# A new order table for a two-layer linear-attention and gated-GLU kernel, with the masks and the activation-table load moved in its first microseconds

## The chip, the cores and the metric

One core of a Trainium2 chip runs the whole program. The metric is device time in microseconds (us) of one execution. The kernel before took 378.02 us (median of three runs, 377.85 to 378.40).

## The reference

The input `x` is 2048 rows of 512 bfloat16 numbers. Four stages follow one another, each added to its own input: A, B, A, B, with the same weights both times.

```
x = x + A(layernorm(x));  x = x + B(layernorm(x));  x = x + A(layernorm(x));  x = x + B(layernorm(x))

A: q, k, v = x @ wqkv                       # 32 heads of 16
   phi(u)  = [softmax(u @ w_phi), softmax(-(u @ w_phi))]      # 32 features a head
   kv = sum over s of phi(k)^T v;   z = sum over s of phi(k)
   o  = (phi(q) kv) / (phi(q) z + 1e-6);    result = o @ wo
B: result = (relu(x @ W_gate) * (x @ W_up)) @ W_down          # width 1376
```

## The kernel before, in words

The 2048 rows are 16 tiles of 128 rows by 512, held in `X` on the chip for the whole run; four tiles make a chunk. The work on one tile is a chain of small operations over five engines: TensorE (PE) multiplies, VectorE (DVE), ScalarE (ACT) and GpSimd (POOL) do what lies between, SyncE (SP) issues transposing DMAs and loads. All line numbers are those of the kernel before; in the changed kernel the lines of the functions shown here stand 7 to 35 further down, those of the key and query stages 33.

**Stage A of layer 0, keys.** A layernorm's statistics are `bn_stats` and `bn_aggr` on DVE (L331, L333), some 128x2 operations on POOL (L339, L341, L389, L391: the power to -1/2 is L341), and the normalising operation on ACT (L403), DVE or POOL (L415). The normalised tile is transposed. PE makes `k` through `w_phi` (L653, four matmuls) and `v` (L606). ACT takes the exponential of + and - of it (L674) into `ek`. The sums of each head's features come from DVE alone (L625 over both halves, L635 over one), or from POOL adding one half's pairs first (L622, here called a half) and DVE the rest (L631). DVE inverts the sums (L683, `rk`). Then `ek` is multiplied by `rk` (L688, here called the scale): a table `ks` says for each tile how many of its eight groups of four heads POOL does, the rest is DVE's. So a tile of 128x1024 elements is one operation on one of these engines, or one on each. PE sums the scaled features times `v` over all 16 tiles (L711). After the last tile DVE masks the result into `R` (L733, two operations).

**Queries and outputs.** Queries go the same way (L753, L757, sums at L622 to L635, L762, L766, a scale at L773, a transposing DMA at L775). When `R` stands, PE multiplies each query tile by it (L792, called er here); its result has one buffer, so each er waits until DVE has read the one before (L810 and L812). The output is transposed (by PE at L832, or by DMA), multiplied by `wo` (L843) and added to `X` (L509). Nothing of stage B starts before that.

**Stage B** takes gate and up (L556), the activations (L562 to L573), a rest of 96 columns (L536 to L546), the down product (L588) and the addition to `X` (L513). In layer 0 each finished tile goes straight into the statistics, the keys and the queries of layer 1, so the stages overlap.

**What sets the order.** Python builds one list of 1881 operations in program order (`Plan.op`). `ORDER`, a table of 1881 numbers written into the file, says in what order they are given out (`emit`). Each engine runs its own share of that list strictly in that order, and waits at an operation until its inputs are there and its buffer is free. The table `STEP` says by a letter or a digit which engine does an operation. Numbers such as `occ`, `lat` and `at` in `Plan.op` do not reach the chip.

**The start.** Two loads of `X` are issued on SP, five loads on ACT's queue (`LOAD_ACT`), then the activation that makes ACT load its exponential table (L172). Until the first statistics DVE fills constants. The masks `M8` and `M4` (L198, L200) are made from constants that POOL prepares; `M8` is needed for the block-diagonal `Wblk` (L270), `M4` for `R`. PE multiplies zeros 20 times (L261), then transposes and folds the key weights (L294, L307), which ACT or DVE copies out (L250, L252, table `wev`).

Of the kernel before, what the change touches and what calls it, by code (L numbers as in the profile page):

```python
# [8 lines left out]
P = 128  # L9
D = 512  # L10
# [7 lines left out]
EPS = 1e-5  # L18
# [32 lines left out]
class Plan:  # L51
# [65 lines left out]

NV = 8
# [3 lines left out]
WF_IN, WK_IN, WV_IN, WQ_IN, LOADED = 3.5, 5.95, 10.0, 14.1, 13.0  # L122
X_IN = [3.27, 3.85] + [7.2] * 2 + [8.5] * 4 + [11.4] * 4 + [12.8] * 4
# [8 lines left out]
def setup(ctx, tc, A_x, A_wqkv, A_w_phi, A_wo, B_W_gate, B_W_up, B_W_down, out):  # L132
# [32 lines left out]
    for what in LOAD_ACT:  # L165
        load(nc.scalar, what)
# [5 lines left out]
    nc.scalar.activation(out=wake[:], in_=st.zero[:, 0:1], func=AF.Exp)  # L172
    M8f = const.tile([P, 8], F32, name="M8f")
# [24 lines left out]
    nc.vector.tensor_copy(out=M8[:], in_=M8f[:])  # L198
    st.M4 = const.tile([P, 4], BF16, name="M4")
    nc.vector.tensor_reduce(out=st.M4[:], in_=ident[:].rearrange("p (k h) -> p h k", h=4), axis=AX.X, op=Alu.max)  # L200
# [45 lines left out]
def evacuate(st, eng, ends, on_dve, **deps):  # L246

    nc, pl = st.nc, st.pl
    if eng == "A":
        pl.op("ACT", 0.475, lambda: nc.scalar.copy(out=ends()[0], in_=ends()[1]), **deps)  # L250
    else:
        pl.op("DVE", on_dve, lambda: nc.vector.tensor_copy(out=ends()[0], in_=ends()[1]), **deps)  # L252

# [59 lines left out]
class Norm:  # L313
# [8 lines left out]
    def add(self, t):  # L322
# [8 lines left out]
        pl.op("DVE", 0.597, dur=0.69, fn=lambda: nc.vector.bn_stats(out=bn[:], in_=st.X[:, t, :]), reads=[("X", t)] + ([("Xin", t)] if self.at else []), writes=[(bn, 0)],  # L331
# [448 lines left out]
def attention(st, c, pT, norm, L):  # L780
# [72 lines left out]
    "tB0": "A---", "tB1": "---A", "tA": "----", "wev": "DDDAAAAADDDAAAAA", "xn1": "APAPDAADPAAPAAAA",  # L853
    "turn": "AAADDAAD", "wake": 20, "fuse0": "AFAA", "fuse1": "FFFF", "gate": 3, "sA": 3, "xB0": "ADAADDDADDDAAAAA",
# [5 lines left out]
}  # L860
ORDER = [int(i) for i in """
# [119 lines left out]
def kernel(  # L981
# [4 lines left out]
    with tc.manual_schedule():  # L986
        st.pl.emit()
# [30 lines left out]
```

## Time and profile before

| | us |
|---|---|
| runs: median (lowest, highest) | 378.02 (377.85, 378.40) |
| the profiled execution, its time | 377.86 |
| its span, first to last instruction | 376.1 |
| PE busy | 368.5 |
| DVE busy | 262.5 |
| ACT busy | 212.5 |
| POOL busy | 136.5 |

The profiled execution is 0.16 us under the median, and 1.76 us of it lie outside the span. The granted TensorE clock is 0.999 throughout. A row of the timeline gives the start and the length of an instruction, or of several of one kind in a row (x2, x3); in brackets is how long the engine was idle before it and what it waited for. Neighbouring rows of DVE overlap by 0.06 to 0.1 us, so a length is slightly more than the place it takes. A row of the waits says which line of which engine waited for whom: the total, how often, the longest.

### The profile page before, as it was taken

How to read it: one execution, taken by the hardware profiler on the slowest of the kernel's cores; microseconds unless marked ns; L12 is line 12 of the kernel's file. 1: busy time of each engine (PE TensorE's matmuls, PEld its weight loads, DVE VectorE, ACT ScalarE, POOL GpSimd, SP SyncE). 2: the span in 40 equal slices, each digit the busy share in tenths (PEclk: the TensorE clock that was granted, in tenths of full speed). 3: DMA queues.
4: the chain of work that ended last, by engine and by line, in shares of the span. 5: the costliest groups of instructions: out<-in, count | busy, mean ns of one | idle time of the engine just before them, and what ended most of it. 6: DMA issues, size and time to landing. Idle time of an engine off the chain costs nothing.

```text
span 376.1 us, 6927 instructions
## 1 busy us (share of the span) xinstructions
PE 368.5 (98%) x2530; PEld 196.6 (52%) x2530; DVE 262.5 (70%) x608; ACT 212.5 (57%) x478; POOL 136.5 (36%) x223
## 2 busy tenths in 40 slices
PE   8999998999999999999999999999999999999996
PEld 4455445877644545444444446566655454444453
DVE  7999999998879854267554976898875353325343
ACT  4999898767745537784666264786522352042100
POOL 6999998362410028024601765431410011000000
PEclk9999999999999999999999999999999999999999
DMA  8898565675843823400140032266583321000031
GB/s 267 178 194 186 139 147 99 116 108 120 133 93 63 120 43 71 98 0 2 29 92 7 15 58 44 49 121 127 119 136 84 58 62 24 0 14 2 0 110 60
DMA packets 95746, 31.83 MB, mean 85 GB/s; under 512 B 87424, under 2 KB 95200, under 8 KB 95712
## 3 DMA queue, kind: packets, MB, share of 16 engines
q1 hardware_dynamic: 93024, 27.97, 38.4%
q10 hardware_dynamic: 2688, 3.42, 2.7%
q8 instruction: 20, 0.33, 0.4%
q14 instruction: 14, 0.11, 0.1%
HBM read 8.44 MB, written 2.10 MB: 28 GB/s over the span
## 4 chain that ended last, share of the span: by engine, by line
PE 83%; DVE 12%; ACT 1%; DMA 1%; POOL 1%; issue 1%
PE ps L556 37%; PE ps L588 20%; PE ps L843 7%; PE ps L753 4%; PE ps L653 4%; PE ps L536 3%; PE ps L606 3%; DVE b L688 3%; PE q L792 2%; DVE sk L625 2%; DVE rk L683 2%; PE ps L261 1%; DVE sk L635 1%; DMA b<-b 1%; PE q L711 1%; DVE bnst L331 1%
## 5 line engine op out<-in xcount | busy, mean ns | idle before, releaser
L566 ACT ACTIVATE b<-ps 128x512 bf16<-128x512 f32 (+3 forms) x110 | 50.4, 482 | 68.1 <-PE ps L556 67.8
L556 PE MATMUL ps<-b,wu 128*128 128x512 bf16 (+3 forms) x440 | 82.1, 321 | 0.2 <-ACT sq L491 0.2
L556 PE MATMUL ps<-b,wg 128*128 128x512 bf16 (+3 forms) x440 | 81.5, 321 | 0.0
L588 PE MATMUL ps<-wd,b 128*128 128x512 bf16 (+4 forms) x374 | 79.2, 366 | 0.0
L588 PEld LDWEIGHTS <-b 128*128 128x128 bf16 (+1 forms) x374 | 35.3, 98 | 39.3
L556 PEld LDWEIGHTS <-wg 128*128 128x128 bf16 x440 | 38.5, 98 | 31.6
L556 PEld LDWEIGHTS <-wu 128*128 128x128 bf16 x440 | 38.4, 98 | 31.0 <-issue 0.5
L622 POOL TENSOR_TENSOR b<-b 128x256 f32<-128x256 bf16 x39 | 27.5, 718 | 62.8 <-ACT b L757 33.5
L569 DVE SCALAR_TENSOR_TENSOR b<-ps,b 128x512 bf16<-128x512 f32 (+2 forms) x60 | 34.1, 593 | 22.6 <-PE ps L556 12.2
L757 ACT ACTIVATE b<-ps 128x512 bf16<-128x512 f32 x64 | 37.3, 642 | 8.9 <-PE ps L753 7.6
L674 ACT ACTIVATE b<-ps 128x512 bf16<-128x512 f32 x64 | 37.7, 645 | 5.9 <-PE ps L653 5.4
L688 POOL TENSOR_TENSOR b<-b,rk 128x1024 bf16<-128x1024 bf16 (+6 forms) x26 | 36.7, 1424 | 7.5 <-DVE rk L683 4.4
L513 DVE SCALAR_TENSOR_TENSOR X<-ps,r,X 128x512 bf16<-128x512 f32 (+2 forms) x22 | 14.9, 694 | 27.7 <-PE ps L588 27.7
L653 PE MATMUL ps<-Wk,b 128*128 128x512 bf16 x128 | 32.2, 379 | 0.6 <-ACT b L250 0.3
L843 PE MATMUL ps<-wo,b 128*128 128x512 bf16 x128 | 32.7, 379 | 0.0
L753 PE MATMUL ps<-Wq,b 128*128 128x512 bf16 x128 | 32.0, 379 | 0.0
L606 PE MATMUL ps<-wkv,b 128*128 128x512 bf16 x128 | 31.8, 379 | 0.0
L509 DVE SCALAR_TENSOR_TENSOR X<-ps,X 128x512 bf16<-128x512 f32 x32 | 21.7, 679 | 7.4 <-PE ps L843 7.4
L562 ACT ACTIVATE b<-ps 128x128 bf16<-128x128 f32 (+2 forms) x50 | 20.5, 430 | 8.9 <-PE ps L556 8.4
L573 DVE TENSOR_TENSOR b<-b,b 128x128 bf16<-128x128 bf16 (+2 forms) x50 | 15.0, 332 | 14.8 <-ACT b L562 9.8
L773 POOL TENSOR_TENSOR b<-b,rq 128x512 bf16<-128x512 bf16 x21 | 22.1, 1056 | 0.7
L812 DVE TENSOR_TENSOR b<-q,dd 128x512 bf16<-128x512 f32 x32 | 21.8, 683 | 0.6
(94 smaller groups left out, 482.7 us busy)
## 6 DMA issues: line engine op xcount, KB each, us to landing
out_dram<-X SPq DMA_DIRECT2D x15, 128.0 KB, 1.9
X<-in_A_x_dram ACTq DMA_DIRECT2D x3, 512.0 KB, 6.6
b<-b SPq DMA_TRANSPOSE x91, 3.1
wg<-in_B_W_gate_dram SPq DMA_DIRECT2D x8, 160.0 KB, 2.7
wu<-in_B_W_up_dram SPq DMA_DIRECT2D x8, 160.0 KB, 3.2
wd<-in_B_W_down_dram SPq DMA_DIRECT2D x5, 256.0 KB, 3.2
wkv<-in_A_wqkv_dram ACTq DMA_DIRECT2D x2, 512.0 KB, 5.9
wq<-in_A_wqkv_dram ACTq DMA_DIRECT2D x1, 512.0 KB, 4.0
```

Source lines behind the costliest of these rows:

```text
L556: nc.tensor.matmul(ps[:], lhsT=wt[:, b, f * P:(f + 1) * P], rhs=xnT[:, lo:hi, b, :], start=(b == 0), stop=(b == NDB - 1))
L566: pl.op("ACT", 0.045 + 0.43 * share, lambda ups=ups, ru=ru, sign=1.0 if fuse else -1.0: nc.scalar.activation(out=ru[:], in_=ups[:], func=A ...
L569: pl.op("DVE", 0.058 + 0.548 * share, dur=0.138 + 0.548 * share, fn=lambda gps=gps, ru=ru, h=h, cs=cs: nc.vector.scalar_tensor_tensor(out= ...
L588: nc.tensor.matmul(yps[:], lhsT=hs[f][:fsz, ti * P:(ti + 1) * P], rhs=st.wd[:fsz, f, cols], start=(f == 0), stop=(f == NFT - 1))
L606: nc.tensor.matmul(vp[:], lhsT=xnT[:, ti, kb, :], rhs=st.wkv[:, kb, D:2 * D], start=(kb == 0), stop=(kb == NDB - 1))
L622: nc.gpsimd.tensor_tensor(out=h[:].rearrange("p j h f -> p j f h"), in0=x[:, :, 0], in1=x[:, :, 1], op=Alu.add)
L653: nc.tensor.matmul(ps[:], lhsT=xnT[:, ti, kb, :], rhs=w(kb), start=(kb == 0), stop=(kb == NDB - 1))
L674: pl.op("ACT", 0.48, lambda s=s, ek=ek, pk=pk: nc.scalar.activation(out=ek[:, :, s, :], in_=pk[:].rearrange("p (j x) -> p j x", j=8), func ...
L688: eng.tensor_tensor(out=phiK[:, lo:hi, :, :].rearrange("p j s (f h) -> p (j s) f h", h=4), in0=ek[:, lo:hi, :, :].rearrange("p j s (f h) - ...
L753: nc.tensor.matmul(pq[:], lhsT=xnT[:, ti, kb, :], rhs=st.Wq2[:, kb, :], start=(kb == 0), stop=(kb == NDB - 1))
L757: pl.op("ACT", 0.48, lambda s=s, eq=eq, pq=pq: nc.scalar.activation(out=eq[:, :, s, :], in_=pq[:].rearrange("p (j x) -> p j x", j=8), func ...
L843: nc.tensor.matmul(yps[:], lhsT=turned(b), rhs=st.wo[:, b, :], start=(b == 0), stop=(b == NDB - 1))
```

## The change

`ORDER` is a new table, now of 1885 numbers: the same operations in another order, with the two masks as operations in it. As numbers it tells a reader nothing. The replay is able to add waits between operations, from a table `BEHIND`; that table is empty, so none is added. The masks come ahead of the first `bn_stats`, which now names `M4` as an input. Three loads stay ahead of the table load on ACT's queue (f, k and tiles 2 and 3), two come behind it (tiles 4 to 7, v). `STEP` has changes in five entries, and a new entry `st` whose other letter, "A", no tile uses. The landing times are numbers of the planning only.

```diff
-    def emit(self):
+    def emit(self, tc):
         for o in self.order():
...
             o.fn()
+            o.ins = tc.nc.cur_bb.bb.instructions[-1]
+            for v in BEHIND.get(o.i, ()):
+                tc.add_manual_dep(o.ins, self.ops[v].ins.name, mybir.DependencyInfo(mybir.DependencyClass.Sync, mybir.DependencyReason.ANTI),
+                                  reason="one at a time on the port that VectorE and GpSimd share")
...
+BEHIND = {}
...
-    for what in LOAD_ACT:
+    for what in LOAD_ACT[:3]:
         load(nc.scalar, what)
...
     nc.scalar.activation(out=wake[:], in_=st.zero[:, 0:1], func=AF.Exp)
+    for what in LOAD_ACT[3:]:
+        load(nc.scalar, what)
...
-    nc.vector.tensor_copy(out=M8[:], in_=M8f[:])
-    nc.vector.tensor_reduce(out=st.M4[:], in_=ident[:].rearrange("p (k h) -> p h k", h=4), axis=AX.X, op=Alu.max)
...
+def masks(st):
...
+    pl.op("DVE", 0.1, lambda: nc.vector.tensor_copy(out=st.M8[:], in_=st.M8f[:]), writes=[("M8", 0)], at=2.75)
+    pl.op("DVE", 0.17, lambda: nc.vector.tensor_reduce(
+        out=st.M4[:], in_=st.ident[:].rearrange("p (k h) -> p h k", h=4), axis=AX.X, op=Alu.max), reads=[("M8", 0)], writes=[("M4", 0)], at=2.75)
...
-    "tB0": "A---", "tB1": "---A", "tA": "----", "wev": "DDDAAAAADDDAAAAA", "xn1": "APAPDAADPAAPAAAA",
+    "tB0": "A---", "tB1": "---A", "tA": "----", "wev": "ADADAAAADDDAAAAA", "xn1": "APAPDAADPAAPAAAA",
-    "turn": "AAADDAAD", "wake": 20, "fuse0": "AFAA", "fuse1": "FFFF", "gate": 3, "sA": 3, "xB0": "ADAADDDADDDAAAAA",
+    "xB0": "ADAAADAADADADADD", "xB1": "DDAAAAAAAADDDDAD", "xA": "ADDADDADDDDAADAD", "xm0": "11222111",
-    "xB1": "DDAAAAAAAADDDDAD", "xA": "ADDADDDADAADADAD", "xm0": "11222111", "xmB0": "12221222", "xmB1": "22121122",
-    "ks0": "6087060714860850", "ks1": "3484716308718788", "kr0": "2H2P11H11PH21HH1", "kr1": "21221HP12P1H212H",
+    "ev0": "AAAAAAAAAAAAAAAA", "ev1": "DAAAAAADAAAAADAD", "ks0": "6087160714860850", "ks1": "3484716308718788",
-    "qr0": "P2H1H2HPPH2P2H12", "qr1": "21P2111HHH2P1H1P", "qs0": "PPPPPPPPDPDDPDPP", "qs1": "DDPDDPDPPPPPDPDP",
+    "qs0": "PPPPPPPPPPDPPDPP", "qs1": "DDPDDPDPPPPPDPDP", "qq0": "PPPPPPPPPPDPPPPP", "qq1": "DDPDPDDDPPPPDPPP",
...
-3 4 5 108 109 110 111 112 113 114 115 116 117 118 7 6 138 8 134 0 9 12 13 14 15 129 128 139 135 16 130 142 131 140
+3 4 5 6 110 111 112 113 114 7 9 8 10 115 116 117 118 119 120 121 14 136 140 15 130 131 132 16 17 21 137 0 144 11 12 1
...
 def layers(st):
     NC, pl = st.NC, st.pl
     load_weights(st)
+    masks(st)
```

Three places show what the table moves. A name such as `b_409` is a buffer, with a number of its own in each program; `sk` are sums, `rk` their inverses.

The first place is on DVE, in the keys of layer 0, before: the scale of tile 3 (`b_428`, 128x128, the seven other parts being POOL's), then those of tile 6 (`b_475`) and tile 5 (`b_505`).

```order
L683 RECIPROCAL rk_749<-sk_533 128x64
L688 TENSOR_TENSOR b_428<-b_427,rk_611 128x128
L683 RECIPROCAL rk_762<-sk_711 128x64
L688 TENSOR_TENSOR b_475<-b_474,rk_749 128x1024
L688 TENSOR_TENSOR b_505<-b_504,rk_762 128x256
```

The same place of DVE in the change: tile 3's scale (`b_409`), the sums of tile 5, tile 6's scale (`b_469`), and tile 4's (`b_428`), which POOL now shares.

```order
L716 RECIPROCAL rk_664<-sk_510 128x64
L721 TENSOR_TENSOR b_409<-b_408,rk_618 128x128
L658 TENSOR_REDUCE sk_713<-b_500 128x64
L721 TENSOR_TENSOR b_469<-b_468,rk_664 128x1024
L721 TENSOR_TENSOR b_428<-b_427,rk_512 128x896
```

Tile 5's scale has left this place; tile 4's, which before stood eight places ahead of tile 3's, now stands behind tile 6's. On POOL the scale of all of tile 2 stood behind tile 3's; it now stands ahead of it.

The second place is some 10 us later, on DVE before: the scales of tile 8 (`b_639`), tile 7 (`b_542`) and tile 9 (`b_555`).

```order
L683 RECIPROCAL rk_818<-sk_801 128x64
L635 TENSOR_REDUCE sq_816<-b_647 128x8x4
L688 TENSOR_TENSOR b_639<-b_638,rk_811 128x896
L762 RECIPROCAL sq_816<-sq_816 128x8x4
L688 TENSOR_TENSOR b_542<-b_541,rk_809 128x128
L631 TENSOR_REDUCE sq_847<-b_709 128x8x4
L688 TENSOR_TENSOR b_555<-b_554,rk_818 128x512
```

On DVE in the change: tile 8 (`b_585`), tile 5 (`b_501`), tile 7 (`b_522`), a sum, tile 9 (`b_609`).

```order
L716 RECIPROCAL rk_757<-sk_752 128x64
L795 RECIPROCAL sq_750<-sq_750 128x8x4
L721 TENSOR_TENSOR b_585<-b_584,rk_747 128x896
L721 TENSOR_TENSOR b_501<-b_500,rk_723 128x256
L721 TENSOR_TENSOR b_522<-b_521,rk_734 128x128
L668 TENSOR_REDUCE sq_847<-b_634 128x8x4
L721 TENSOR_TENSOR b_609<-b_608,rk_757 128x512
```

POOL at the second place in the change: its parts of tile 7 (`b_522`), tile 5 (`b_501`) and tile 8 (`b_585`), halves (L655), and the scale of query tile 0 (`b_602`).

```order
L721 TENSOR_TENSOR b_522<-b_521,rk_734 128x896
L721 TENSOR_TENSOR b_501<-b_500,rk_723 128x768
L655 TENSOR_TENSOR b_759<-b_700 128x8x8x4
L799 TENSOR_TENSOR rq_805<-sq_750 128x32
L721 TENSOR_TENSOR b_585<-b_584,rk_747 128x128
L806 TENSOR_TENSOR b_602<-b_602,rq_805 128x8x64
```

So at the second place three scales of DVE now stand one behind the other and a fourth behind one sum, beside POOL's parts of the same tiles; before it was three scales, with a short operation between each two.

The third place is on DVE where layer 0 ends: tile 13's addition to `X` (`ps_3443`), its statistics, and its normalising operation (`b_3484`), before.

```order
L513 SCALAR_TENSOR_TENSOR X<-ps_3443,r_3039,X 128x512
L331 BN_STATS bnst_3465<-X 128x6
L333 BN_AGGR mv_3467<-bnst_3465 128x2
L762 RECIPROCAL sq_3459<-sq_3459 128x8x4
L688 TENSOR_TENSOR b_2915<-b_2914,rk_3094 128x256
L766 TENSOR_TENSOR rq_3477<-sq_3459 128x32
L415 TENSOR_SCALAR b_3484<-X,mv_3467,rstd_3473 128x512
```

In the change tile 13's addition (`ps_3383`) comes ahead of tile 14's (`ps_3397`).

```order
L546 SCALAR_TENSOR_TENSOR X<-ps_3383,r_3131,X 128x512
L364 BN_STATS bnst_3409<-X 128x6
L546 SCALAR_TENSOR_TENSOR X<-ps_3397,r_3131,X 128x512
L366 BN_AGGR mv_3420<-bnst_3409 128x2
L364 BN_STATS bnst_3475<-X 128x6
L658 TENSOR_REDUCE sq_3477<-b_3269 128x64
L721 TENSOR_TENSOR b_3281<-b_3280,rk_3328 128x896
L366 BN_AGGR mv_3480<-bnst_3475 128x2
L448 TENSOR_SCALAR b_3482<-X,mv_3420,rstd_3473 128x512
```

PE follows the same order: before, tile 13's down product was the last of layer 0; now it is the last but one, with tile 14's 11 matmuls behind it. Between tile 13's down product and its key product (L653) PE had 8 key and value products of four matmuls and 8 matmuls of L711 before; in the change it has tile 14's down product, 10 key and value products and 16 matmuls of L711.

More of the change, by code (lines that the diff above doesn't have):

```diff
@@ L121 @@
 LATE = ((8, 12), (12, 16), "q")
-WF_IN, WK_IN, WV_IN, WQ_IN, LOADED = 3.5, 5.95, 10.0, 14.1, 13.0
-X_IN = [3.27, 3.85] + [7.2] * 2 + [8.5] * 4 + [11.4] * 4 + [12.8] * 4
+WF_IN, WK_IN, WV_IN, WQ_IN, LOADED = 3.57, 5.83, 10.1, 14.03, 13.0
+X_IN = [3.35, 4.26] + [6.46] * 2 + [8.61] * 4 + [11.37] * 4 + [12.62] * 4
 TINY = 0.165
@@ L252, in evacuate @@
         pl.op("DVE", on_dve, lambda: nc.vector.tensor_copy(out=ends()[0], in_=ends()[1]), **deps)
+def masks(st):
+    nc, pl = st.nc, st.pl
+    pl.rank("w")
+    pl.op("DVE", 0.1, lambda: nc.vector.tensor_copy(out=st.M8[:], in_=st.M8f[:]), writes=[("M8", 0)], at=2.75)
+    pl.op("DVE", 0.17, lambda: nc.vector.tensor_reduce(
+        out=st.M4[:], in_=st.ident[:].rearrange("p (k h) -> p h k", h=4), axis=AX.X, op=Alu.max), reads=[("M8", 0)], writes=[("M4", 0)], at=2.75)
 def wake(st):
@@ L329, in add @@
             return self.add_sums(t, n)
+        by_act = self.at is not None and n == 1 and STEP["st"][t] == "A"
+        if by_act:
+            e2, nv, rstd = Buf("u", [P, 4], F32), Buf("ve", [P, 4], F32), Buf("rstd", [P, 4], F32)
+            for out, func, scale in ((lambda: e2[:, 0:1], AF.Square, D ** -0.5), (lambda: mv[:, 0, 0:1], AF.Identity, 1.0 / D)):
+                junk = Buf("sq", [P, D], BF16)
+                pl.op("ACT", 0.67, lambda out=out, func=func, scale=scale, junk=junk: nc.scalar.activation(
+                    out=junk[:], in_=st.X[:, t, :], func=func, scale=scale, accum_out=out()),
+                    reads=[("X", t), ("Xin", t)], writes=[(junk, 0), (e2, 0) if func == AF.Square else (mv, 0)], at=self.at[t])
+            pl.op("POOL", TINY, lambda: nc.gpsimd.tensor_scalar(
+                out=nv[:, 0:1], in0=mv[:, 0, 0:1], scalar1=mv[:, 0, 0:1], scalar2=e2[:, 0:1], op0=Alu.mult, op1=Alu.subtract),
+                reads=[(mv, 0), (e2, 0)], writes=[(nv, 0)])
+            pl.op("POOL", TINY, lambda: nc.gpsimd.tensor_scalar(
+                out=nv[:, 0:1], in0=nv[:, 0:1], scalar1=-1.0, scalar2=EPS, op0=Alu.mult, op1=Alu.add), reads=[(nv, 0)], writes=[(nv, 0), ("stat", t)])
+            pl.op("POOL", 0.39 + 0.155, lambda: nc.gpsimd.tensor_tensor(out=rstd[:, 0:1], in0=nv[:, 0:1], in1=st.mhalf[:, 0:1], op=Alu.pow),
+                  reads=[(nv, 0)], writes=[(rstd, 0)])
+            self.tiles.append(t)
+            return self.normalise(n, mv, rstd)
         bn = Buf("bnst", [P, 6], F32)
-        pl.op("DVE", 0.597, dur=0.69, fn=lambda: nc.vector.bn_stats(out=bn[:], in_=st.X[:, t, :]), reads=[("X", t)] + ([("Xin", t)] if self.at else []), writes=[(bn, 0)],
+        pl.op("DVE", 0.597, dur=0.69, fn=lambda: nc.vector.bn_stats(out=bn[:], in_=st.X[:, t, :]), reads=[("X", t)] + ([("Xin", t), ("M4", 0)] if self.at else []), writes=[(bn, 0)],
               at=self.at[t] if self.at else 0.0)
@@ L852 @@
     "raw": 0, "kev": "ADAD", "pp0": "1111111111111111", "pp1": "1111111111111111", "part0": "3111", "part1": "6111",
-    "tB0": "A---", "tB1": "---A", "tA": "----", "wev": "DDDAAAAADDDAAAAA", "xn1": "APAPDAADPAAPAAAA",
-    "turn": "AAADDAAD", "wake": 20, "fuse0": "AFAA", "fuse1": "FFFF", "gate": 3, "sA": 3, "xB0": "ADAADDDADDDAAAAA",
[5 rows of a table removed]
+    "tB0": "A---", "tB1": "---A", "tA": "----", "wev": "ADADAAAADDDAAAAA", "xn1": "APAPDAADPAAPAAAA",
+    "st": "DDDDDDDDDDDDDDDD", "turn": "AAADDAAD", "wake": 20, "fuse0": "AFAA", "fuse1": "FFFF", "gate": 3, "sA": 3,
[6 rows of a table added]
 }
 ORDER = [int(i) for i in """
[72 rows of a table removed]
[72 rows of a table added]
 """.split()]
@@ L986 @@
     with tc.manual_schedule():
-        st.pl.emit()
+        st.pl.emit(tc)
 _INS = ['A_x', 'A_wqkv', 'A_w_phi', 'A_wo', 'B_x', 'B_W_gate', 'B_W_up', 'B_W_down']
```

147 rows, old and new, of tables (ORDER, STEP) are left out of this document.

## The prediction

> **What bounds the kernel now.** First the page's busy shares, the windows by stage, and the waits of PE.
>
> ```profile
> PE 368.5 (98%) x2530; PEld 196.6 (52%) x2530; DVE 262.5 (70%) x608; ACT 212.5 (57%) x478; POOL 136.5 (36%) x223
> ...
> 15.00:60.00 45.00, 42.91 (x338) 22.41 (x336) 44.39 (x88) 41.70 (x82) 42.17 (x55) 1.00 0.71 150
> ...
> 80.00:220.00 140.00, 140.00 (x825) 72.22 (x823) 96.74 (x237) 83.55 (x192) 45.46 (x88) 1.00 0.34 63
> ...
> PE q L711 <- POOL b L688: 1.1, 2, 0.9
> ...
> PE q L792 <- DVE R L733: 0.3, 1, 0.3
> PE ps L653 <- ACT b L250: 0.3, 1, 0.3
> ```
>
> The columns of a window are its length, then the busy time of PE, PE's weight loads, DVE, ACT and POOL. PE is busy 368.5 of 376.1 us, so no order of the same matmuls can win more than the 7.6 us between them. The stages differ. From 80 to 220 us PE has no idle time at all: what DVE, ACT and POOL do there costs nothing while it comes in time. From 15 to 60 us DVE is busy 44.39 of 45 us, PE 42.91: there **DVE is the bound**. All keys of layer 0 must be scaled before `R`, and PE has no work that could go ahead of the first er without limit. So a microsecond more on DVE before `R` is a microsecond more at the end, and one less is a gain until PE's idle time there is used up, 45.00 - 42.91 = 2.1 us and the piece of the wait for L250 at 10.6, some 2.4 together.
>
> Inside those 45 us DVE's work is itself stretched. These are rows of the timeline of DVE, then of POOL.
>
> ```profile
> 26.35 1.16 DVE L688 TENSOR_TENSOR b<-b,rk 128x1024 bf16<-128x1024 bf16 x1
> ...
> 27.77 0.28 DVE L688 TENSOR_TENSOR b<-b,rk 128x256 bf16<-128x256 bf16 x1
> ...
> 28.75 0.62 DVE L688 TENSOR_TENSOR b<-b,rk 128x1024 bf16<-128x1024 bf16 x1
> ...
> 30.88 0.15 DVE L688 TENSOR_TENSOR b<-b,rk 128x128 bf16<-128x128 bf16 x1
> ...
> 31.42 2.54 DVE L688 TENSOR_TENSOR b<-b,rk 128x1024 bf16<-128x1024 bf16 x2
> ...
> 40.06 1.48 DVE L688 TENSOR_TENSOR b<-b,rk 128x896 bf16<-128x896 bf16 x1
> ...
> 41.73 0.42 DVE L688 TENSOR_TENSOR b<-b,rk 128x128 bf16<-128x128 bf16 x1
> ...
> 42.41 0.95 DVE L688 TENSOR_TENSOR b<-b,rk 128x512 bf16<-128x512 bf16 x1
> ...
> 54.50 1.55 DVE L688 TENSOR_TENSOR b<-b,rk 128x1024 bf16<-128x1024 bf16 x2
> ...
> 58.13 0.77 DVE L733 TENSOR_TENSOR R<-M,q 128x272 bf16<-128x272 bf16 x2
> ```
>
> ```profile
> 25.49 1.48 POOL L688 TENSOR_TENSOR b<-b,rk 128x768 bf16<-128x768 bf16 x1
> ...
> 31.04 1.69 POOL L688 TENSOR_TENSOR b<-b,rk 128x896 bf16<-128x896 bf16 x1
> 32.70 1.12 POOL L622 TENSOR_TENSOR b<-b 128x256 f32<-128x256 bf16 x1
> 33.77 1.96 POOL L688 TENSOR_TENSOR b<-b,rk 128x1024 bf16<-128x1024 bf16 x1
> ...
> 44.68 1.05 POOL L773 TENSOR_TENSOR b<-b,rq 128x512 bf16<-128x512 bf16 x1
> ```
>
> A whole tile's scale takes DVE 0.62 us alone (28.75). The same took 1.16 at 26.35, when POOL's scale of 25.49 ran until 26.97, and the pair at 31.42 took 2.54 where 0.62 + 0.28 = 0.90 would do, less 0.08 of overlap. DVE's scale ends about half a microsecond after the POOL operation it met: it **waits for it**. It goes the other way too: the half at 32.70 took 1.12, as it lay beside the end of DVE's first scale, and held up the second. The excess over the lone lengths is 0.54 at 26.35, 1.72 at 31.42, 0.9 at 40.06 (lone about 0.55, seven eighths of 0.62), 0.27 at 41.73, 0.6 at 42.41 (lone about 0.35) and 0.73 at 54.50 (a pair of 1024 and 256 again): 4.8 us in all.
>
> The Trainium skill, on the page "SBUF — State Buffer" under "Who interferes with whom", says that a DVE operation with two inputs in this memory and a GpSimd one that reads it share a port pair, held by whoever issues first for its whole instruction. The rows above agree for long POOL operations; the rivals come back to it.
>
> **The change part by part.** The sum is made against the profiled execution (377.86 us), 0.16 under the median.
>
> *Nothing: the waits.* The table from which `emit` would add waits is empty; what DVE waited for POOL before was the hardware's doing, and it stays so.
>
> *Masks.*
>
> ```profile
> 3.38 0.69 DVE L331 BATCH_NORM_STATS2 bnst<-X 128x6 f32<-128x512 bf16 x1 [0.60 <-DMA X<-in_A_x_dram]
> ...
> 5.12 0.25 DVE L200 TENSOR_REDUCE M<-ident 128x4 bf16<-128x128 bf16 x1
> 5.29 0.16 DVE L198 CAST M<-M8f 128x8 bf16<-128x8 f32 x1
> ...
> 6.58 1.18 DVE L252 COPY b<-ps 128x512 bf16<-128x512 bf16 x3 [0.34 <-PE ps L294]
> ...
> 1.47 0.19 POOL L177 TENSOR_SCALAR_AFFINE_SELECT M8f<-M8f 128x8 f32<-128x8 f32 x1
> ```
>
> Both take 0.41 us, fit into DVE's idle 0.60 before the first tile lands, and POOL has their inputs ready at 1.66. DVE gets 0.4 us earlier to `Wblk`, then waits 0.4 longer for PE's transposes at 6.58: I take 0. Without that cover it is worth -0.4 to +0.1. One copy of the weights goes from DVE to ACT, where that engine waits too: the bounds are the one L250 wait of PE gone (-0.3) or doubled (+0.3), 0 taken.
>
> *Table load between the issues.*
>
> ```profile
> 3.63 1.28 ACT L172 ACT_TABLE_LOAD   x1 [3.63 <-issue]
> 3.70 0.47 ACTq L162 DMA_DIRECT2D X<-in_A_x_dram  x1
> 5.99 0.81 ACT L403 ACTIVATE b<-X,ve,rstd 128x512 bf16<-128x512 bf16 x1 [0.86 <-POOL ve L391]
> ```
>
> A load was issued at 3.70 while the table load ran, so the table load doesn't hold the queue, and ACT's first real work waits for POOL until 5.99. With the load of v and tiles 4 to 7 behind the wake-up instead of ahead of it, the worst is one 1.28 us delay of tiles 4 to 7, whose statistics DVE reaches late enough to lose about 0.3 of it. I take 0, bounds 0 and +0.3.
>
> *The order of layer 0's keys.* DVE's operations ahead of `R` are the same in number and kind but for those just told and one small eighth of tile 4 that POOL takes, and PE has 406 matmuls ahead of the first er in both orders, so what can differ is how long scales wait. I followed both engines' new rows with the lone lengths above and the rule that a scale waits for the POOL operation running, and a waiting one goes first when the other ends:
> - tile 0's quarter on DVE now comes while POOL does its own three quarters (1.48, released by the same reciprocal): 1.2 us, between 0.9 and 1.48. Before, tile 0's quarter at 27.77 met nothing, and tile 4's paid 0.54.
> - tile 6 meets the tail of tile 2's 1.96 on POOL: 0.75, between 0 and 1.96; tile 4 behind it nothing, and a DVE sum idles 0.4 for a half that POOL starts later. Before, the two scales here paid 1.72.
> - tile 8 waits 0.2 for POOL's 1.69 to end. Then POOL's three quarters of tile 5 (1.48), waiting, go ahead of DVE's quarter of tile 5: 1.45. Tile 7's eighth waits for the half behind (0.65), and tile 9 for tile 0's query scale (1.05): 0.95. Together 3.25, between 1.0 if DVE's three go in one run and 4.4 if each meets a whole operation. Before: 0.9 + 0.27 + 0.6 = 1.8.
> - tiles 12, 14, 11 and 15: POOL's last scales are done by then: 0, up to 1. Before: 0.73.
>
> After: 1.2 + 0.75 + 0.4 + 3.25 = 5.6. Before: 4.8. **+0.8**, between -2.4 (PE's idle time, the most that can be won) and +3 (next part). `R` then starts near 58.9 instead of 58.13.
>
> *60 to 220 us.* The new letters move whole operations of 0.3 to 0.8 us between DVE and ACT. PE's 140.00 of 140 covers them, DVE having 43 us and ACT 56 us to spare in that window: 0. If the cover failed at one place it would be one such length, +0.8.
>
> *The end of layer 0.* PE's row with the stall, and how tile 13 came to it:
>
> ```profile
> 214.56 2.54 PE L588 MATMUL ps<-wd,b 128*128 128x512 bf16 x11
> ...
> 217.13 0.75 DVE L513 SCALAR_TENSOR_TENSOR X<-ps,r,X 128x512 bf16<-128x512 f32 x1 [0.44 <-PE ps L588]
> ...
> 219.98 0.41 DVE L415 TENSOR_SCALAR b<-X,mv,rstd 128x512 bf16<-128x512 bf16 x1 [0.67 <-POOL rstd L341]
> ...
> 222.37 1.03 PE L653 MATMUL ps<-Wk,b 128*128 128x512 bf16 x4
> 223.23 1.03 PE L606 MATMUL ps<-wkv,b 128*128 128x512 bf16 x4
> 224.49 1.04 PE L653 MATMUL ps<-Wk,b 128*128 128x512 bf16 x4 [0.23 <-DMA b<-b]
> ...
> 240.72 0.43 PE L792 MATMUL q<-R,b 128*128 128x68 bf16 x8 [0.31 <-DVE b L812]
> ```
>
> From tile 13's down product (ends 217.1) to its key product 7.4 us pass, and PE had only 8 products in between, at 0.86 each (222.37 to 223.23), and 8 short matmuls (0.3): the key product could have started at 223.23 + 0.86 = 224.09 and started at 224.49, a stall of 0.4 (0.23 of it shown as idle). Now PE has a down product (2.4), 10 products (8.6) and 16 short matmuls (0.5) there, 11.5 us, so the chain is hidden with 4 us to spare: **-0.4**. Tile 14, now last, has about 10 us of work behind it. Bounds -0.4 and 0. The stall at 240.72 stays: one er waits for the output of the one before, with one product between them; its neighbours change places, and I find about the same 0.5 again. Behind 256 us PE has only stage B: 0.
>
> **Sum:** 377.86 + 0.8 - 0.4 = 378.26; against the median 0.16 more, **378.4**.
>
> **The rivals.** A measurement of this kernel can tell about 0.2% (0.76 us) from no change.
>
> *The waits fall kindly (faster).* The list of waits is a guess at who comes first, each time by a few tenths. If the scales of tiles 8, 5 and 7 run in one piece, and tile 0's waits little, 1.6 to 3.2 us of the 5.6 go, the last of them at the limit of PE's idle time: -0.8 to -2.4 in front, -0.4 behind, 375.2 to 376.8. For it: these three stand together now, so that a POOL operation may be waited for once instead of three times. Against: POOL is itself busy 42.17 of 45 us, so a DVE scale that meets no POOL operation is rare.
>
> *A whole POOL scale in the wrong place (slower).* In the change tile 2's scale on POOL (1024 wide, 1.96) stands ahead of tile 3's, and tile 3's eighth on DVE (0.15 alone) comes at nearly the same time. If POOL is first, DVE waits up to 1.96 with everything behind it, and up to 1.1 more where a half slips in as at 32.70: +1.9 to +3. It decides within some 0.3 us of arrival. Then 380.3 to 381.4. For it: POOL has 1 us more to do than before ahead of tile 14's scale (a half more, and tile 4's eighth), so it comes later to all that stands behind. Against: in my walk DVE comes first.
>
> *Short POOL operations block too (slower by less).*
>
> ```profile
> 14.95 0.40 DVE L415 TENSOR_SCALAR b<-X,mv,rstd 128x512 bf16<-128x512 bf16 x1
> 14.91 0.71 POOL L341 TENSOR_TENSOR rstd<-ve,mhalf 128x2 f32<-128x2 f32 x1
> ```
>
> Here DVE took its usual 0.40 beside POOL's power of 0.71, so such operations seem not to block. That DVE row has one wide input, though, the scale two. If the scale does wait, tile 4's comes upon the power that now follows tile 2's scale: +0.7, 379.1. The same section of the Trainium skill would have it so, as it makes no difference of length; on the row above that rule does not hold.
>
> *The order does nothing.* If both orders lose the same in waits and the stall at 224 turns up elsewhere: 377.8 to 378.3.
>
> **How the numbers follow.** Forecast 40% (377.2 to 379.6: 0.03 faster, 0.20 same, 0.17 slower); kind waits 25% (faster); POOL's whole scale 20% and the short operations 8% (slower); nothing 7% (same). So 0.28 faster, 0.27 same, 0.45 slower. The range reaches half into the kind waits and nearly through the slow case: 376.0 to 381.3, which leaves out about 2 in 10.
>
> **What would show it.** Right: `R` on DVE starting at 58.5 to 59.5; a long tile 5 quarter near 41 (1.7 instead of 0.28); PE in the window 15 to 60 about 42 busy; no DMA wait at L653's successor. Wrong: `R` before 58 (kind waits), a 128x128 scale of 2 us near 30 (POOL first), a PE wait between 80 and 220, or the first key product after 11.2.

## The result, and the profile after

The changed kernel takes 376.63 us (median of 17 runs), the kernel before 378.09 (17 runs): a ratio of 0.9967, 95% interval 0.9958 to 0.9975, so 1.2 us faster by the ratio of the means (1.5 by the medians), and clear of no change. The forecast was 378.4, 0.1% slower. The time lies inside the stated range, but on the other side. A few executions of the study took 481 to 1375 us, among them the profiled ones of experiments 1 and 12; no ratio and no reading below rests on them.

The changed kernel's windows, and all waits of its PE:

```profile
15.00:60.00 45.00, 42.72 (x334) 22.02 (x332) 43.73 (x87) 41.27 (x81) 41.78 (x55) 1.00 0.68 154
...
80.00:220.00 140.00, 140.00 (x831) 72.44 (x829) 99.35 (x234) 82.32 (x192) 46.99 (x89) 1.00 0.35 62
PE q L744 <- DVE b L721: 1.7, 1, 1.7
PE ps L277 <- DVE zero L177: 1.2, 1, 1.2
PE ps L323 <- DVE b L259: 0.5, 1, 0.5
PE ps L639 <- ACT b L707: 0.3, 1, 0.3
PE ps L865 <- DVE b L845: 0.3, 1, 0.3
```

The front looks as before: DVE nearly full, PE 2.3 us short of the window. What is missing from the list are the small waits of the back: no key product waits for a DMA, no er for the output before it, no up product (L556 before) for ACT. (In the front, PE's waits at L711 of 1.1 and 0.6 have become one of 1.7.)

Three landmarks in PE's timeline divide the run: the first er of layer 0, the first er of layer 1, and the end. Of before, then of the change:

```profile
59.04 0.41 PE L792 MATMUL q<-R,b 128*128 128x68 bf16 x8 [0.29 <-DVE R L733]
...
235.15 0.43 PE L792 MATMUL q<-R,b 128*128 128x68 bf16 x8
```

```profile
58.94 0.41 PE L825 MATMUL q<-R,b 128*128 128x68 bf16 x8
...
234.41 0.41 PE L825 MATMUL q<-R,b 128*128 128x68 bf16 x8
```

| stretch | before | change | measured | forecast |
|---|---|---|---|---|
| start to first er, layer 0 | 59.04 | 58.94 | -0.10 | +0.8 |
| to first er, layer 1 | 176.11 | 175.47 | -0.64 | -0.4 |
| to the end (376.1, 374.8) | 140.95 | 140.39 | -0.56 | 0 |

The gain isn't where the forecast looked for a loss. It lies behind `R`, in stalls of PE of 0.1 to 0.5 us each. The rows of the last stretch, before (up to the er at 240.72) and in the change:

```profile
239.38 1.02 PE L843 MATMUL ps<-wo,b 128*128 128x512 bf16 x4
```

```profile
239.48 1.03 PE L786 MATMUL ps<-Wq,b 128*128 128x512 bf16 x4
240.35 0.42 PE L825 MATMUL q<-R,b 128*128 128x68 bf16 x8
...
241.46 0.39 PE L511 MATMUL ps<-ident,b 128*128 128x128 bf16 x4
241.94 0.43 PE L825 MATMUL q<-R,b 128*128 128x68 bf16 x8
```

Before, the er at 240.72 could have started 0.86 after the product at 239.38, at 240.24: a stall of 0.48. Now the er at 240.35 has an earlier product ahead of it and starts on time; the next has four transposes (0.22) more between, and stalls 241.94 - 241.68 = 0.26. And the stall of an up product at 253 is gone:

```profile
252.71 0.38 PE L556 MATMUL ps<-b,wg 128*128 128x128 bf16 x4
253.25 1.46 PE L556 MATMUL ps<-b,wu 128*128 128x384 bf16 x8 [0.15 <-ACT sq L491]
```

```profile
251.73 0.39 PE L589 MATMUL ps<-b,wg 128*128 128x128 bf16 x4
251.95 0.81 PE L589 MATMUL ps<-b,wu 128*128 128x384 bf16 x4
```

In the row of before 0.54 us lie between the starts where the change needs 0.22: 0.32. Together 0.22 + 0.32 = 0.54 of the 0.56.

**The key scales.** DVE's rows of the change that answer to those of the prediction, then POOL's:

```profile
25.72 0.97 DVE L721 TENSOR_TENSOR b<-b,rk 128x256 bf16<-128x256 bf16 x1
...
28.81 0.16 DVE L721 TENSOR_TENSOR b<-b,rk 128x128 bf16<-128x128 bf16 x1
...
30.01 2.12 DVE L721 TENSOR_TENSOR b<-b,rk 128x1024 bf16<-128x1024 bf16 x2
...
36.05 0.42 DVE L664 TENSOR_REDUCE sq<-b 128x32 f32<-128x256 f32 x1 [0.38 <-POOL b L655]
...
38.04 2.83 DVE L721 TENSOR_TENSOR b<-b,rk 128x896 bf16<-128x896 bf16 x3
...
41.39 1.25 DVE L721 TENSOR_TENSOR b<-b,rk 128x512 bf16<-128x512 bf16 x1
...
55.57 1.09 DVE L721 TENSOR_TENSOR b<-b,rk 128x1024 bf16<-128x1024 bf16 x3
...
58.01 0.78 DVE L766 TENSOR_TENSOR R<-M,q 128x272 bf16<-128x272 bf16 x2
```

```profile
25.06 1.88 POOL L721 TENSOR_TENSOR b<-b,rk 128x768 bf16<-128x768 bf16 x2
...
28.23 0.72 POOL L374 TENSOR_TENSOR rstd<-ve,mhalf 128x2 f32<-128x2 f32 x1
...
29.14 1.91 POOL L721 TENSOR_TENSOR b<-b,rk 128x1024 bf16<-128x1024 bf16 x1
31.00 1.16 POOL L374 TENSOR_TENSOR rstd<-ve,mhalf 128x2 f32<-128x2 f32 x1
...
36.59 3.52 POOL L721 TENSOR_TENSOR b<-b,rk 128x896 bf16<-128x896 bf16 x2
```

By the lone lengths of the prediction the excess is 0.69 at 25.72, 1.03 at 30.01 (1024 and 896, alone 0.62 + 0.55 - 0.08), 2.0 at 38.04 (896, 256 and 128, alone 0.82), 0.9 at 41.39 and nothing at 55.57: 4.6 us, against 4.8 before. The long quarter of tile 5 and its neighbours came as forecast; `R` came at 58.01 and not at 58.9.

### The profile page after: what moved, and what is told of

Same layout as the page of the kernel before. It is cut to its first block, busy times and chain, and to the rows that moved or that the text cites. A ratio compares the mean times of both kernels' runs of the same rounds, so it can differ in the third digit from the quotient of the medians.

```text
span 374.8 us, 6931 instructions
## 1 busy us (share of the span) xinstructions
PE 367.1 (98%) x2530; PEld 195.8 (52%) x2530; DVE 264.1 (70%) x606; ACT 210.4 (56%) x478; POOL 139.4 (37%) x226
## 4 chain that ended last, share of the span: by engine, by line
PE 83%; DVE 8%; POOL 6%; DMA 1%; issue 1%; ACTq 0%
PE ps L589 37%; PE ps L621 20%; PE ps L876 7%; PE ps L786 4%; PE ps L686 4%; PE ps L639 4%; PE ps L569 3%; PE q L825 2%; DVE bnst L364 2%; POOL b L721 1%; PE q L744 1%; DMA X<-in_A_x_dram 1%; DVE b L721 1%; POOL b L655 1%; POOL b L448 1%; DVE rk L716 1%
## 5 line engine op out<-in xcount | busy, mean ns | idle before, releaser
L721 POOL TENSOR_TENSOR b<-b,rk 128x1024 bf16<-128x1024 bf16 (+6 forms) x27 | 38.2, 1427 | 24.1 <-DVE rk L716 15.3
L790 ACT ACTIVATE b<-ps 128x512 bf16<-128x512 f32 x64 | 35.8, 618 | 14.3 <-PE ps L786 12.3
L707 ACT ACTIVATE b<-ps 128x512 bf16<-128x512 f32 x64 | 36.4, 637 | 4.2 <-PE ps L686 3.9
L655 POOL TENSOR_TENSOR b<-b 128x256 f32<-128x256 bf16 x39 | 26.7, 701 | 30.8 <-ACT b L790 12.3
L806 POOL TENSOR_TENSOR b<-b,rq 128x512 bf16<-128x512 bf16 x23 | 23.9, 1048 | 0.5
L524 ACT ACTIVATE sq<-b 128x512 bf16<-128x512 bf16 x32 | 20.2, 632 | 6.2 <-DVE b L503 6.0
```

The source lines that it names most:

```text
L655: nc.gpsimd.tensor_tensor(out=h[:].rearrange("p j h f -> p j f h"), in0=x[:, :, 0], in1=x[:, :, 1], op=Alu.add)
L707: pl.op("ACT", 0.48, lambda s=s, ek=ek, pk=pk: nc.scalar.activation(out=ek[:, :, s, :], in_=pk[:].rearrange("p (j x) -> p j x", j=8), func ...
L721: eng.tensor_tensor(out=phiK[:, lo:hi, :, :].rearrange("p j s (f h) -> p (j s) f h", h=4), in0=ek[:, lo:hi, :, :].rearrange("p j s (f h) - ...
L790: pl.op("ACT", 0.48, lambda s=s, eq=eq, pq=pq: nc.scalar.activation(out=eq[:, :, s, :], in_=pq[:].rearrange("p (j x) -> p j x", j=8), func ...
```

## The experiments

The first theory (the prediction's) was that the key scales' waits decide. After the result it was replaced by **"behind R"**: the gain is the sum of PE's small stalls behind `R`. Its rivals are "front" (the start and the keys bring the gain) and, for one run, "start". Every ratio below is against the kernel before on the same chip.

**1. Start alone.** The order and `STEP` of before, with the masks and loads of the change:

```diff
     for what in LOAD_ACT[:3]:
...
     load_weights(st)
+    masks(st)
```

> The kernel before with only the start of the change: masks ahead of the first statistics and the table load between the issues; order and engine table otherwise as before. Theory 'behind R' (what was won lies in PE's waits after R, 60 to 80 and 220 to 256 us): no change, within 0.3 us. Theory 'start' (0.36 us of masks taken out of DVE's full stretch reach the end): 0.4 us faster. R on DVE, which started at 58.13, would start at 57.8 by 'start'.

Measured: 378.20 against 378.18, ratio 0.9998 (0.9989 to 1.0006). The start brings nothing that can be told; the 0.4 us of "start" is at the edge of the interval.

**2. New keys, old rest.** `ORDER` of the change up to `R`, the remaining operations in the order of before:

```diff
-    "tB0": "A---", "tB1": "---A", "tA": "----", "wev": "DDDAAAAADDDAAAAA", "xn1": "APAPDAADPAAPAAAA",
+    "tB0": "A---", "tB1": "---A", "tA": "----", "wev": "ADADAAAADDDAAAAA", "xn1": "APAPDAADPAAPAAAA",
-    "ks0": "6087060714860850", "ks1": "3484716308718788", "kr0": "2H2P11H11PH21HH1", "kr1": "21221HP12P1H212H",
+    "ks0": "6087160714860850", "ks1": "3484716308718788", "kr0": "2H2P11H11PH21HH1", "kr1": "21221HP12P1H212H",
```

> The new order up to R with its letters (wev, ks0), the order and letters of before behind R. 'Behind R': 0.1 us faster than before, as R moves from 58.13 to 58.01 only. Rival 'front' (start and key scales bring the gain): 1.0 to 1.4 us faster. The recorded prediction's term for this part was 0.8 us slower.

Measured: 378.06, ratio 1.0000 (0.9988 to 1.0011). "Front" falls, and so does the prediction's +0.8 (ratio 1.002). Its profiled execution took 379.99, 1.9 above its median, and shows why: DVE and POOL around tile 3's eighth in that execution.

```profile
29.74 1.83 DVE L721 TENSOR_TENSOR b<-b,rk 128x128 bf16<-128x128 bf16 x1
...
32.62 3.06 DVE L721 TENSOR_TENSOR b<-b,rk 128x1024 bf16<-128x1024 bf16 x2
...
60.30 0.79 DVE L766 TENSOR_TENSOR R<-M,q 128x272 bf16<-128x272 bf16 x2
```

```profile
29.58 1.91 POOL L721 TENSOR_TENSOR b<-b,rk 128x1024 bf16<-128x1024 bf16 x1
...
32.43 1.69 POOL L721 TENSOR_TENSOR b<-b,rk 128x896 bf16<-128x896 bf16 x1
```

This is the prediction's slower rival: POOL's scale of tile 2 started 0.16 us ahead, tile 3's eighth took 1.83 instead of 0.16, and tile 6's then met POOL's next one. `R` came 2.3 us after that of the change. The same front may go either way in one execution or another. Behind the first er this execution takes as long as the kernel before, 317.0 us against 317.1.

**3. Old keys, new rest.** The reverse: `wev` and `ks0` of before, the other letters of the change, `ORDER` of before up to `R`.

```diff
-    "xB0": "ADAADDDADDDAAAAA"
+    "xB0": "ADAAADAADADADADD"
-    "xA": "ADDADDDADAADADAD"
+    "xA": "ADDADDADDDDAADAD"
-    "qs0": "PPPPPPPPDPDDPDPP"
+    "qs0": "PPPPPPPPPPDPPDPP"
```

> The order of before up to R (masks and loads as in the change), the new order and letters behind R. 'Behind R': 1.0 to 1.3 us faster than before, PE's stalls at 224, 240 and 253 gone or halved. 'Front': within 0.3 us of before.

Measured: 377.00, ratio 0.9968 (0.9956 to 0.9979), 1.2 us faster: all of the gain. In its trace 175.47 us lie between the two first ers and 140.4 behind them, as in the change. "Behind R" stands.

**4. New order from 205 us on**, letters of before:

```diff
 ORDER = [int(i) for i in """
-(from tile 15's down product of layer 0 on: order of before)
+(from there on: order of the change)
```

> The order of before up to the first down product of tiles 12 to 15 (about 205 us), the new order from there on; letters of before (they agree from there on). 'Behind R' with its main part in the end of layer 0: 0.6 to 0.9 us faster than before, the stall of 0.4 at 224 gone. The recorded prediction's term for this part was 0.4 us faster. 'Front': no change.

Measured: 378.59, ratio 1.0010 (1.0000 to 1.0019): a miss. The two orders don't fit at this seam. PE gets a wait that neither kernel has:

```profile
PE ps L639 <- ACT vext L257: 0.6, 1, 0.6
```

A value product waits for ACT to empty an earlier one, most likely because the values of the old half come to ACT in another order. The stall at 224 is gone and this one stands in its place. The run tells that what was won near 224 needs the order ahead of it as well, not that it was nothing.

**5. Tile 5's scale wholly on DVE**, in the changed kernel:

```diff
-    "ev0": "AAAAAAAAAAAAAAAA", "ev1": "DAAAAAADAAAAADAD", "ks0": "6087160714860850", "ks1": "3484716308718788",
+    "ev0": "AAAAAAAAAAAAAAAA", "ev1": "DAAAAAADAAAAADAD", "ks0": "6087100714860850", "ks1": "3484716308718788",
```

> The changed kernel, but all of tile 5's key scale on DVE instead of three quarters of it on POOL. DVE gets 0.4 us more work (1024 instead of 256 elements), and the waits of 1.3 (tile 5), 0.5 (tile 7) and part of 0.9 (tile 9) that the trace of the change shows around 38 to 42 us lose their POOL operation. 'Waits reach R one to one': R on DVE 1 to 1.5 us before 58.01, 1.0 to 1.5 us faster than the change (375.2 to 375.7). Rival 'PE has no more to gain in front': R earlier, the end within 0.3 us of the change.

Measured: 375.65, ratio 0.9929 (0.9917 to 0.9941): 1.0 us below the change by the medians, 1.4 by the two ratios, each of which is known to some 0.4 us. DVE does four times as much for tile 5, and is done sooner:

```profile
38.16 2.00 DVE L721 TENSOR_TENSOR b<-b,rk 128x896 bf16<-128x896 bf16 x3
...
57.10 0.79 DVE L766 TENSOR_TENSOR R<-M,q 128x272 bf16<-128x272 bf16 x2
```

Tiles 8, 5 and 7 take 2.00 us, with 1024 elements of tile 5, instead of 2.83 with 256. `R` comes 0.91 earlier and the end 1.0. So the front was the bound as the prediction said, and waits for POOL reach the end one to one; they were only not what the change altered. In the profiles of the change and of experiments 5, 6, 9 and 10, which differ in the keys alone, the first er stands anywhere from 57.75 to 59.23, and the end comes 315.9 behind it each time.

**6. Against the race.** The changed kernel, tile 3's eighth ahead of a reciprocal on DVE:

```diff
-L716 RECIPROCAL rk_664<-sk_510 128x64
 L721 TENSOR_TENSOR b_409<-b_408,rk_618 128x128
+L716 RECIPROCAL rk_665<-sk_510 128x64
 L658 TENSOR_REDUCE sk_713<-b_500 128x64
```

> The changed kernel with one reciprocal on DVE moved behind tile 3's eighth, so that this scale comes 0.45 us earlier, some 0.8 instead of 0.33 us ahead of POOL's scale of tile 2. The race of the recorded prediction (POOL first costs 1.9 to 3 us): no run above the median by more than 1 us, where the change had 2 of 17 and the kernel with only the new key order had a profiled run with a 1.83 us scale there. Median as the change, within 0.3. If the slow runs have another cause, they stay.

Measured: 376.43, ratio 0.9948 (0.9936 to 0.9959); 5 runs from 376.17 to 376.69. No run was high, but 2 of 17 in the change would leave none in 5 about half the time ((15/17)^5 = 0.53). Inconclusive on the race; the median is as expected.

**7. Tiles 13 and 14 swapped** in the kernel before, and tile 13's normalising earlier on DVE:

```diff
-L513 SCALAR_TENSOR_TENSOR X<-ps_3443,r_3039,X 128x512
-L331 BN_STATS bnst_3465<-X 128x6
-L333 BN_AGGR mv_3467<-bnst_3465 128x2
-L762 RECIPROCAL sq_3459<-sq_3459 128x8x4
+L546 SCALAR_TENSOR_TENSOR X<-ps_3443,r_3039,X 128x512
+L364 BN_STATS bnst_3463<-X 128x6
+L366 BN_AGGR mv_3465<-bnst_3463 128x2
+L448 TENSOR_SCALAR b_3467<-X,mv_3422,rstd_3426 128x512
+L795 RECIPROCAL sq_3457<-sq_3457 128x8x4
```

(The names at the line numbers of the kernel before and of the changed file; `ps_3443` is now tile 14's.)

> The kernel before (with the masks and loads of the change, which make no difference) with one edit: tiles 13 and 14 change places in the down products, additions and statistics, and tile 13's normalising comes earlier on DVE. 'The stall at 224 reaches the end': 0.4 us faster, no DMA wait at that key product. Rival 'it turns up elsewhere': same time, another wait within the next 10 us.

Measured: 379.17, ratio 1.0016 (1.0006 to 1.0026): slower. The stall at 224 is gone, but ACT, then PE, show a new one:

```profile
220.62 0.81 ACT L436 ACTIVATE b<-X,ve,rstd 128x512 bf16<-128x512 bf16 x1 [3.04 <-POOL ve L424]
221.34 1.06 ACT L707 ACTIVATE b<-ps 128x512 bf16<-128x512 f32 x2
```

```profile
222.46 1.02 PE L639 MATMUL ps<-wkv,b 128*128 128x512 bf16 x3 [1.06 <-ACT b L707]
```

ACT now stands at tile 14's normalising, whose statistics come last, with tile 15's ready exponentials queued behind it; PE's next value product waits 1.06 for a result buffer that those exponentials have to read first. That is 0.83 more than the idle 0.23 it replaces, and the kernel is 0.6 us slower (0.2 to 1.0).

**8. New tail.** `ORDER` of before up to `R` of layer 1 (some 232 us), of the change behind it, letters of before:

```diff
 ORDER = [int(i) for i in """
-(behind R of layer 1: order of before)
+(behind R of layer 1: order of the change)
```

> The order of before up to R of layer 1 (about 232 us), the order of the change behind it; letters of before. 'Behind R' by the list of PE's stalls: those of 0.48 at 240 and 0.32 at 253 become 0.25 and 0: 0.4 to 0.5 us faster than before. The recorded prediction had them unchanged: 0.

Measured: 377.91, ratio 0.9988 (0.9978 to 0.9998): 0.45 us, the size expected, but only in part by the stalls expected. In its trace the stall of 0.48 has become 0.26 (at 243.47 here), as in the change. The one at 253 is still there:

```profile
253.25 0.39 PE L589 MATMUL ps<-b,wg 128*128 128x128 bf16 x4
253.83 0.81 PE L589 MATMUL ps<-b,wu 128*128 128x384 bf16 x4 [0.20 <-DMA b<-b]
```

The second row could have started 0.22 behind the first, at 253.47: 0.36 late. The stretch from the first er of layer 1 (235.92) to the end (376.7) is 140.78, only 0.2 less than before. The rest of the 0.45 lies within the interval. The profiled execution took 378.41, and has a DMA wait of 0.5 near 79.6 that neither kernel shows.

**9. Every wait edit of the keys at once**, in the changed kernel:

```diff
-    "ks0": "6087160714860850"
+    "ks0": "6087100804860850"
```

with the edit of experiment 6.

> The changed kernel with all edits that take a wait out of the key scales: tiles 5 and 8 wholly on DVE, tile 7 wholly on POOL, tile 3's eighth ahead of a reciprocal. Against the kernel with tile 5 alone (375.65, R at 57.10) DVE loses tile 7's eighth (0.15) and its wait (0.4) and gains an eighth (0.07): 'waits reach R one to one' gives R 0.4 to 0.6 us earlier and 375.0 to 375.3. Rival 'PE or another engine is the bound by now': 375.5 to 375.7.

Measured: 375.55, ratio 0.9935 (0.9923 to 0.9947), against 375.65 of experiment 5: a miss. In its profile `R` starts at 56.81, 0.3 before that of experiment 5, less than the 0.4 to 0.6 expected, as tile 0's quarter took 1.33 in this execution and 0.97 in that of experiment 5. The spans, 373.6 and 373.9, differ by the same 0.3. PE's waits add up to as much as there. This is the fastest version of the study by median, though it can't be told from experiment 5.

**10. Forcing the race.** The changed kernel, tile 4's scale ahead of tile 3's eighth on DVE:

```diff
+L721 TENSOR_TENSOR b_428<-b_427,rk_512 128x896
 L721 TENSOR_TENSOR b_409<-b_408,rk_618 128x128
 L658 TENSOR_REDUCE sk_714<-b_500 128x64
 L721 TENSOR_TENSOR b_469<-b_468,rk_664 128x1024
-L721 TENSOR_TENSOR b_428<-b_427,rk_512 128x896
```

> The changed kernel with one edit: tile 4's scale on DVE (0.55) comes ahead of tile 3's eighth, so that POOL's scale of tile 2 (1.91) is waiting by then and goes first, as in the profiled run of the kernel with the new keys alone. The recorded rival 'a whole POOL scale in the wrong place': tile 3's eighth takes 1.8 to 2 us, R comes 1.9 to 2.4 us later, 378.4 to 379.0. If that race is harmless: 376.4 to 376.8.

Measured: 376.69, ratio 0.9965 (0.9953 to 0.9977): a miss, but not because the race is harmless. It didn't take place:

```profile
28.82 0.68 DVE L721 TENSOR_TENSOR b<-b,rk 128x896 bf16<-128x896 bf16 x2
```

```profile
28.95 0.51 POOL L422 TENSOR_SCALAR u<-mv 128x2 f32<-128x2 f32 x1
29.42 1.91 POOL L721 TENSOR_TENSOR b<-b,rk 128x1024 bf16<-128x1024 bf16 x1
```

DVE's two scales ran from 28.82 to 29.50 (0.68, alone 0.62). POOL's short operation ahead of its scale, 0.24 in the change, took 0.51, and its scale came only as DVE was done. The price of the race rests on experiment 2's execution alone.

**11. New middle.** Order of before up to `R`, of the change up to `R` of layer 1, of before behind it; letters as in experiment 3.

```diff
 ORDER = [int(i) for i in """
-(between R of layer 0 and R of layer 1: order of before)
+(between R of layer 0 and R of layer 1: order of the change)
```

> Only the middle of the new order: order of before up to R (58 us), of the change up to R of layer 1 (232 us), of before behind it. What the new order gained behind R (1.2) less what its tail alone gained (0.45) is left: 0.65 to 0.8 us faster than before, by the stalls of 0.4 at 224 and 0.25 between 62 and 80. If the parts don't add up: 0 to 0.4.

Measured: 377.11, ratio 0.9973 (0.9963 to 0.9983), 1.0 us. Its first er and that of layer 1:

```profile
59.11 0.41 PE L825 MATMUL q<-R,b 128*128 128x68 bf16 x8 [0.29 <-DVE R L766]
...
234.56 0.42 PE L825 MATMUL q<-R,b 128*128 128x68 bf16 x8
```

175.45 us between, as in the change (175.47), 0.66 less than before. The time moved by more than that, and the trace shows why: behind the first er of layer 1 there are 375.2 - 234.56 = 140.64 us, 0.3 less than before, although the order there is the old one. The stall at 240 is as before (0.48), but the one at 253 is gone, the second row following the first after 0.22:

```profile
252.12 0.38 PE L589 MATMUL ps<-b,wg 128*128 128x128 bf16 x4
252.34 1.46 PE L589 MATMUL ps<-b,wu 128*128 128x384 bf16 x8
```

So that stall hung on the order (or the letters) of the middle; by which operation isn't shown. By the traces, the middle is worth 0.66 + 0.3 and the tail 0.2, together the 1.2 of experiment 3; the 1.0 and 0.45 of the runs add up to more, within the intervals.

**12. Experiment 7 mended**: tile 14's normalising on ACT behind tile 15's exponentials.

```diff
-L436 ACTIVATE b_3483<-X,ve_3475,rstd_3473 128x512
 L707 ACTIVATE b_3501<-ps_3503 128x8x64 x2
+L436 ACTIVATE b_3509<-X,ve_3475,rstd_3473 128x512
```

> As the kernel with tiles 13 and 14 swapped, which put a new wait of 1.06 us (ACT at tile 14's normalising, ahead of tile 15's exponentials) in place of the stall at 224; here tile 14's normalising stands behind those exponentials. 'The stall at 224 reaches the end one to one': 0.4 us faster than before. Rival 'that place has no slack for any order of these tiles': same as before or slower.

Measured: 377.86, ratio 0.9989 (0.9977 to 1.0001): 0.4 us faster as expected, but the interval just includes no change; 1.0 us faster than experiment 7 by the two ratios. So the loss of experiment 7 hung on one operation on another engine. That tile 13's wait is gone here, and worth its 0.4 us, agrees with the time but isn't shown.

## Why the prediction was wrong, step by step

- **What bounds the kernel**: right. PE's 140 of 140 stayed; DVE's front sets `R`, and what is taken off it arrives at the end (experiment 5: 0.91 at `R`, 0.9 in the span, 1.0 in the medians).
- **Masks, table load, empty table at nothing**: right within 0.4 us (experiment 1).
- **Keys, "+0.8"**: this step failed, and by the most. The trace has -0.1 at the first er, the runs 0 (-0.45 to +0.4, experiment 2). Term by term: tile 0's quarter 0.69, not 1.2; tiles 6 and 4 1.03, not 0.75; the idle sum 0.38, as forecast 0.4; tiles 8, 5, 7 and 9 2.9, not 3.25; the last tiles 0 as forecast. That makes 5.0, not 5.6, against 4.8: +0.2 by waits. The rest lies in what was taken as equal or at 0. Counted from start to start until `R`, DVE spends 9.49 us on scales before and 9.09 in the change, 45.34 and 44.78 on everything else, and is idle for 2.38 and 3.23: -0.40, -0.56 and +0.85, together -0.1. The weights copy that ACT now does, taken at 0, is -0.50 of it. DVE's new idle times are 0.95 at 6.70, for a load of `X`, and 0.48 at 22.78, for ACT, besides the 0.38; three waits for PE, 0.85 in all, are gone. Two rows of DVE's waits in the change, the first with the 0.6 ahead of the first tile in it:

```profile
DVE bnst L364 <- DMA X<-in_A_x_dram: 1.5, 2, 0.9
...
DVE sk L658 <- ACT b L707: 0.5, 1, 0.5
```

One pair of traces doesn't settle a few tenths: in six profiled executions with the old keys (before, and experiments 3, 4, 7, 8 and 11) the first er stood between 58.89 and 59.30, the two ends being the rows below, of experiments 7 and 8. But experiment 2 excludes 0.8. That scales wait for POOL was right; the term was a difference of two sums of ten races, each known to a few tenths, and its sign was not to be had from it.

```profile
58.89 0.41 PE L825 MATMUL q<-R,b 128*128 128x68 bf16 x8 [0.29 <-DVE R L766]
```

```profile
59.30 0.38 PE L825 MATMUL q<-R,b 128*128 128x68 bf16 x7 [0.29 <-DVE R L766]
```

- **"60 to 220 us ... 0" and "the end of layer 0, -0.4"**: 0.64 was won between the two first ers. The stall of 0.40 at 224 went, as forecast. The other 0.24 is in starts of matmuls too close for the profile to list a wait: before, they come 0.07 to 0.1 late at 68.50, 70.28 and 78.72, and in the change none between 60.6 and 80 does. The last of the three, where four matmuls of 0.056 end at 78.62:

```profile
78.40 0.39 PE L556 MATMUL ps<-b,wg 128*128 128x128 bf16 x4
78.72 1.04 PE L843 MATMUL ps<-wo,b 128*128 128x512 bf16 x4
```

That is 0.25, and smaller pieces add 0.08; against them the first er of layer 1 now starts 0.27 late instead of 0.18. So the 0 for this stretch was off by a quarter of a microsecond, which a busy share, 19.68 of 20 us from 60 to 80 in both kernels, doesn't show.
- **"The stall at 240.72 stays ... about the same 0.5 again"**: failed. It went from 0.48 to 0.26, by the new tail, since experiment 8 has the 0.26 too. The error was to follow one chain (er, output, er) and take its length as given, without counting the transposes and products that the new order puts between. The stall at 253 (0.32), which the prediction hadn't priced at all, went altogether, and not by the tail: it stays in experiment 8 and is gone in experiment 11.
- **Rivals**: "kind waits" had the right time, 375.2 to 376.8, for a reason that did not occur, since `R` moved by 0.1 only. "A whole POOL scale in the wrong place" exists (experiment 2's execution, 2.3 us at `R`), and two of the change's 17 runs, 378.23 and 378.28, may be it. "Short POOL operations block too" falls: tile 3's eighth took 0.16 at 28.81 while POOL's power ran from 28.23 to 28.95, and 0.15 at 28.93 in experiment 5, wholly beside a power of 28.36 to 29.08 (0.23 at 28.65 in experiment 6, beside one of 28.38 to 29.10). Here the rule of the Trainium skill ("SBUF — State Buffer", "Who interferes with whom") holds for long POOL operations and not for these.

## What to carry to other kernels

Where one engine is busy to 98%, list its stalls one by one, by the starts of its operations and not by its busy share, and ask of each whether the new order leaves it; a handful of 0.1 to 0.5 us decided here, and the full engine beside it did not. The difference of two sums of many small races between two engines has an error larger than itself: use such a sum to find an edit (tile 5's scale, 1.0 us), not to forecast one. And moving an operation forward on one engine moves what is queued on the others: experiments 4 and 7 each lost their gain to a wait that neither kernel had.

## What the runs showed of the hardware

POOL waits for DVE's scales even with its shortest operations: a power of 128x2 took 1.16 at 31.00 beside a scale and 0.72 at 28.23, a 128x2 `u` 0.51 instead of 0.24 (experiment 10). The reverse doesn't hold in the rows at hand: the scale at 28.81 took its 0.16 beside a power. So beside long operations both wait, beside these short ones only POOL does.
